# First attention of a two-stage kernel: transposed scores and narrower tiles

## The chip, the cores and the metric

The kernel runs on one core of a Trainium2 chip. The metric is the device time of one execution in microseconds; the time before is the median of two runs. The span of a profile is shorter than the time by what lies around it.

## The reference

For 8 batches and 8 heads, with 576 tokens and 64 columns a head, 32 packed queries p attend over the tokens, and the tokens' queries q attend over the 32 results. The output of all heads, x (576 x 512 a batch), goes through a token mixer:

```python
def sm_attn(qq, kk, vv):
    s = scale * np.matmul(qq, kk.transpose(0, 1, 3, 2))
    a = softmax(s)
    return np.matmul(a, vv)
p_packed = sm_attn(p, k, v)
x = sm_attn(q, p_packed, p_packed)      # heads side by side, [8, 576, 512]
wq, wk = x @ w_q, x @ w_k               # 512 -> 64
W_tok = scale * wq @ wk.T
out = np.maximum(W_tok @ x, 0.0) @ w_out
```

Inputs and output are fp32; the kernel works in bf16 with fp32 sums.

## The kernel before, in words

There is no loop over tiles: the string ORDER lists every step as NAME.batch.part@engine=banks, and the program issues them in just that order. Each engine runs its own steps strictly in the order of the list, so a step that waits holds up all later steps of its engine. A is ScalarE (ACT), V VectorE (DVE), P GpSimd (POOL); steps without an engine are TensorE's, with their PSUM banks after the equals sign. Batches run interleaved, in the order 0, 1, 2, 4, 3, 5, 6, 7. All loads of k, q, v (LD.k3 and so on) and of w_out (LD.O) are issued from POOL's queue, stores (ST, STF) from SP's, and their places stand in the same list. WARM steps are matmuls on zeros that keep the TensorE busy early on.

Four heads lie on the 128 partitions of a k or q tile, each head with 32 groups of 18 tokens. One batch goes through these steps:

- KT: a transpose in blocks of 32x32 on DVE turns k to kT (columns of k on partitions). QV does the same for q, in three parts (two of 512 columns, one of 128).
- S1 (line 261): scores of the packed queries, 32 matmuls in 32x32 tiles, p as weights and 288 tokens moving. The 32 packed queries come out on partitions. X1.b.0 and X1.b.1: exponential on ACT, 576 columns each.
- TE.b.0 and TE.b.1 (step TE, by the helper blocks in line 223): DVE transposes the exponentials, so that tokens are on partitions (tile e).
- PV.b.0 and PV.b.1 (line 282): 36 matmuls in 64x64 tiles, the exponentials of two heads as weights, v with columns of ones beside it moving (192 columns). The ones give the sum for the softmax. In the list, steps of other batches stand between the two parts.
- RC, PP (lines 287, 294): reciprocal of the sum, and the result pp scaled by it and laid out by a mask that puts zeros where another head's block is; PT transposes it to ppT.
- QK (line 306) and QKE: pp times the weights w_q and w_k, 4 matmuls of 192 columns (w_k, w_q, and w_q again), copied to pqk.
- S2, X2, RS, RR, AM (lines 339 to 365): scores of q over the 32 results, exponential, sum, reciprocal and product; AT and AE transpose the product by matmuls with an identity and copy it out.
- WKQ, WE (lines 396, 401): wk for the tokens and wq in the other orientation, from pqk. GM, GE, Y, YE (lines 422, 432): the mixer's small product y. MX and MR (lines 446, 452): the mixed tokens; RL, RLF and RLR apply the relu. RL and RLF write their columns in another order than they read them (function turn).
- OT (line 491): product with w_out, 16 matmuls of 512 columns a batch, and 4 more for the remaining 64 tokens of two batches together; OE and OEF copy it out; ST and STF store it.

k, q and v have four buffers each, e1T, e1, kT and the like two.

Of the kernel before, what the change touches and what calls it, by code (L numbers as in the profile page):

```python
# [7 lines left out]
NL, NB, NO, NE = 4, 3, 10, 2  # L8

ORDER = """  # L10
SET.warm LD.P0 LD.P1 LD.P2 LD.P3 LD.W0 LD.W1 LD.K0 LD.k1 LD.K1 SET.mask@V KC.0@V SET.v0@V LD.v0 PC@V
LD.q0 KT.0.0@V KC.1@A SET.v3@V PX@V KT.0.1@V SET.v1@V WARM.27=0 S1.0=0,1,2,3 SET.idf@V KT.1.2@V
SET.aff@P X1.0.1@A LD.k2 WC.0@P SET.aT0@V TE.0.1@V WARM.4=4 S1.1=4,5,6,7 LD.v1 SET.v2@V X1.1.1@A
X1.0.0@A LD.q1 X1.1.0@A TE.0.0@V LD.v2 SET.aT1@V TE.1.1@V WARM.6=2 PV.0.0=2,3 LD.k4 PV.0.1 QV.0.1@V
WC.1@P QV.0.0@V LD.q2 RC.0.1@V RC.0.0@V PP.0.1@V QV.0.2@V PP.0.0@V PT.0@V LD.k3 KT.2.2@V WARM.9=6
S2.0.2=6,7 S2.0.3=0,1 X2.0.2@A X2.0.3@A SET.idb@V TE.1.0@V RS.0.4@V WARM.5=4 PV.1.0=4,5 LD.O PV.1.1
QK.0=2 RC.1.0@V RC.1.1@V RR.0.4@V S1.2=6,7,0,1 PP.1.0@V AM.0.2@P PP.1.1@V AM.0.3@P PT.1@V WARM.1=3
AT.0.2=3 QV.1.1@V AE.0.2@A QK.1=4 X1.2.0@A SET.aT2@V QV.1.0@V QKE.0@A X1.2.1@A QV.1.2@V WARM.2=5
S2.1.3=6,7 LD.v3 QKE.1@A TE.2.1@V S2.1.2=2,3 AT.0.3=5 X2.1.2@A TE.2.0@V X2.1.3@A AE.0.3@V WARM.1=0
PV.2.0=0,1 RS.1.4@V WKQ.0.0=2,3 WKQ.0.2 WKQ.0.1 PV.2.1 WE.0.2@A RR.1.4@V KT.4.2@V AM.1.2@P WARM.1=4  # L20
GM.0=4 AM.1.3@P GE.0@V RC.2.1@V RC.2.0@V WARM.1=6 Y.0=6 PP.2.1@V S1.4=2,3,4,5 YE.0@V PP.2.0@V
X1.4.1@A MX.0.0=6,7 LD.q3 QV.2.0@V MX.0.1=0,1 RL.0.0@A AT.1.3=4 PT.2@V LD.v4 QV.2.1@V AT.1.2=5
X1.4.0@A AE.1.3@V S2.2.3=6,7 RL.0.1@A LD.q4 QV.2.2@V AE.1.2@V S2.2.2=2,3 KT.3.2@V LD.k5 WKQ.1.0=4,5
X2.2.3@A WKQ.1.1 X2.2.2@A WKQ.1.2 S1.3=0,1,6,7 WE.1.2@A RS.2.4@V QK.2=2 X1.3.1@A GM.1=3 LD.q5
OT.0.2=4,5 X1.3.0@A TE.3.1@V GE.1@A OT.0.0=6,7 RR.2.4@V TE.3.0@V OT.0.3 AM.2.2@V AM.2.3@V OT.0.1
LD.k6 OE.0.1@A TE.4.1@V AT.2.2=3 AT.2.3=0 OE.0.0@A AE.2.2@V Y.1=1 TE.4.0@V PV.3.0=4,5 QKE.2@A YE.1@V
MR.0=6,7 PV.3.1 AE.2.3@V RLR.0@A MR.1=2,3 MX.1.0=6,7 LD.v5 RLR.1@A RC.3.1@V QV.3.1@V WKQ.2.0=0,1
RL.1.0@A MX.1.1=2,3 RC.3.0@V WKQ.2.2 PP.3.1@V WKQ.2.1 PP.3.0@V OT.1.4=6 WE.2.2@A PT.3@V QV.3.2@V
QK.3=7 QV.3.0@V OEF.1.4@A GM.2=4 LD.v6 RL.1.1@V PV.4.0=0,1 ST.1.4 GE.2@A QKE.3@A Y.2=6 PV.4.1 YE.2@V
S2.3.2=4,5 S2.3.3=2,3 RC.4.0@V X2.3.2@A RC.4.1@V PP.4.1@V MX.2.0=6,7 OT.1.2=4,5 PP.4.0@V RL.2.0@A  # L30
QV.4.0@V MX.2.1=0,1 X2.3.3@A QV.4.2@V MR.2=6,7 OT.1.3 PT.4@V QV.4.1@V RLR.2@A RL.2.1@A OT.1.0=2,3
RS.3.4@V OE.1.1@A S2.4.2=6,7 S2.4.3=0,1 OT.1.1 RR.3.4@V X2.4.3@A KT.5.2@V AM.3.3@P OT.2.0=4,5
X2.4.2@A OE.1.0@A RS.4.4@V S1.5=0,1,6,7 OT.2.1 LD.q6 X1.5.0@A AM.3.2@V X1.5.1@A LD.k7 AT.3.3=2
RR.4.4@V QV.5.1@V OE.2.0@A OT.2.2=0,1 AM.4.3@P AE.3.3@V QK.4=3 TE.5.1@V AT.3.2=6 OT.2.3 AE.3.2@A
QKE.4@A KT.6.2@V WKQ.3.0=4,5 AM.4.2@P OE.2.1@A AT.4.3=7 LD.v7 WKQ.3.2 WKQ.3.1 AE.4.3@V AT.4.2=6
S1.6=2,3,0,1 WE.3.2@A AE.4.2@V TE.5.0@V WKQ.4.0=6,7 X1.6.1@A QV.5.0@V GM.3=4 LD.q7 WKQ.4.2 X1.6.0@A
WKQ.4.1 GE.3@V PV.5.0=0,1 TE.6.1@V WE.4.2@A Y.3=5 TE.6.0@V PV.5.1 YE.3@A GM.4=4 RC.5.1@V QV.5.2@V
MX.3.1=2,3 RC.5.0@V GE.4@A MX.3.0=6,7 PP.5.0@V RL.3.1@A PV.6.0=4,5 PP.5.1@V Y.4=0 PT.5@V PV.6.1
RL.3.0@A YE.4@V S2.5.3=2,3 RC.6.1@V RC.6.0@V QK.5=1 PP.6.0@V X2.5.3@A PP.6.1@V OT.3.0=6,7 PT.6@V
QKE.5@A S2.5.2=4,5 QV.6.2@V MX.4.0=2,3 QV.6.1@V MR.3=0,1 X2.5.2@A OT.3.1 RL.4.0@A QV.6.0@V RLR.3@V  # L40
S2.6.2=4,5 RS.5.4@V MX.4.1=2,3 S2.6.3=0,1 X2.6.2@A RL.4.1@A OT.3.4=4 X2.6.3@A RR.5.4@V OT.4.0=2,3
OEF.3.4@V AM.5.3@P OE.3.0@A KT.7.2@V QK.6=5 ST.3.4 ST.1.0 OT.4.1 ST.0.0 ST.1.1 ST.0.1 ST.2.0 ST.3.0
OT.3.2=0,1 RS.6.4@V OE.4.0@A AM.5.2@P AT.5.3=4 QKE.6@A ST.4.0 S1.7=6,7,2,3 ST.2.1 RR.6.4@V AE.5.3@V
AT.5.2=5 AM.6.3@P OT.3.3 X1.7.1@A AE.5.2@A X1.7.0@A WKQ.5.0=2,3 OE.3.1@V OT.4.2=4,5 AM.6.2@P WKQ.5.2
WKQ.5.1 QV.7.2@V ST.3.1 TE.7.0@V AT.6.3=6 WE.5.2@A OT.4.3 AE.6.3@V QV.7.1@V GM.5=7 OE.4.1@A
WKQ.6.0=0,1 GE.5@V AT.6.2=6 TE.7.1@V MR.4=2,3 Y.5=7 WKQ.6.1 AE.6.2@A YE.5@A QV.7.0@V WKQ.6.2 RLR.4@A
PV.7.0=4,5 WE.6.2@A MR.5=6,7 MX.5.0=2,3 PV.7.1 RLR.5@V RL.5.0@A MX.5.1=0,1 GM.6=6 RC.7.1@V RC.7.0@V
PP.7.0@V OT.5.4=7 GE.6@A PP.7.1@V RL.5.1@A PT.7@V Y.6=6 OEF.5.4@V S2.7.0=2,3 YE.6@A S2.7.2=4,5
OT.5.2=0,1 X2.7.2@A ST.5.4 ST.4.1 X2.7.0@A RS.7.2@V S2.7.1=6,7 RS.7.0@V MX.6.1=4,5 MX.6.0=2,3
X2.7.1@A OT.5.3 RR.7.2@V RR.7.0@V RL.6.0@A AM.7.2@P RS.7.1@V OT.5.0=6,7 AM.7.0@V OE.5.1@A RR.7.1@V  # L50
RL.6.1@V QK.7=2 AM.7.1@P AT.7.0=3 ST.5.1 OT.5.1 AE.7.0@A QKE.7@V AT.7.2=0 AT.7.1=1 OE.5.0@A AE.7.2@V
WKQ.7.0=4,5 AE.7.1@V MR.6=2,3 WKQ.7.2 WKQ.7.1 ST.5.0 WE.7.0@V OT.6.0=0,1 WE.7.1@A GM.7=6 OT.6.1
GE.7@A RLR.6@A Y.7=7 OT.6.2=4,5 OE.6.0@V YE.7@A MR.7=2,3 MX.7.1=6,7 ST.6.0 MX.7.0=0,1 RLR.7@V OT.6.3
RLF.7.1.0@A RLF.7.0.1@V RLF.7.1.1@A RLF.7.0.0@V OT.7.4=2 OE.6.1@A OT.7.2=3 OEF.7.4@V ST.6.1 OT.7.3=6
ST.7.4 OEF.7.2@V OT.7.1=7 STF.7.2 OEF.7.3@V OT.7.0=0 STF.7.3 OEF.7.1@V STF.7.1 OEF.7.0@A STF.7.0
# [4 lines left out]
def kernel(  # L60
# [27 lines left out]
    P = 128  # L88
# [65 lines left out]
    wqk = const.tile([P, 2, 2, 3, Dl], bf16)  # L154
    wout = const.tile([P, NJ, D], bf16)
    v_bufs = [const.tile([P, 6, W], bf16, name=f"v_sb{n}") for n in range(NL)]
# [33 lines left out]
    mask = const.tile([P, 4, Dh], bf16)  # L190
    aT_bufs = [const.tile([P, 2, 640], bf16, name=f"aT{n}") for n in range(NB)]

    def setup(n):
        a, z = n.rstrip("0123456789"), n[len(n.rstrip("0123456789")):]
        z = int(z or 0)
        if a == "idf":
            zero(idf)
        elif a == "aff":
            nc.gpsimd.affine_select(out=idf, in_=idf, compare_op=mybir.AluOpType.not_equal,
                                    fill=1.0, base=0, pattern=[[-1, P]], channel_multiplier=1)  # L200
        elif a == "warm":
            zero(warm)
        elif a == "idb":
            nc.vector.tensor_copy(idb, idf)
        elif a == "v":
            nc.vector.memset(v_bufs[z][:, 0:6:5].bitcast(u32), 0x3F803F80)  # L206
        elif a == "mask":
            zero(mask.rearrange("a x d -> a (x d)"))
            for u in range(4):
                nc.vector.memset(mask[quarter(u), u, :], 1.0)  # L210
        elif a == "aT":
            for i in range(2):
                zero(aT_bufs[z][:, i, 512:576])
# [24 lines left out]
    def WC(n, eng, bk):  # L238
# [3 lines left out]
        else:  # L242
            copy(eng, wqk[:, :, :, 1], w32[:, 0])
            copy(eng, wqk[:, :, :, 2], w32[:, 0])

    def KT(b, x, eng, bk):
        kT = new("kT", b, [P, 2, RQ, GQ, 2], pool=epool)
        xs = slice(0, 2) if x == 2 else slice(x, x + 1)
        blocks(kT[:, xs].rearrange("a x r g e -> a (x r g e)").bitcast(u32),
               k_in[b][:, xs].rearrange("a x n -> a (x n)").bitcast(u32))  # L250


    def S1(b, eng, bk):
        T["s1", b] = [ps_all[:, n:n + 2, 0:NT] for n in (bk[0], bk[2])]
        for e in range(2):
            for z in range(4):
                for c in range(4):
                    i, gh = (c + z) // 2 % 2, (c + z) % 2
                    lhsT = pT[quarter(c), 2 * b + i, :, e]
                    rhs = T["kT", b][quarter(c), i, :, gh * 16:(gh + 1) * 16, e]  # L260
                    nc.tensor.matmul(T["s1", b][c // 2][quarter(2 * i + gh), c % 2], lhsT, rhs,  # L261
                                     start=e == 0, stop=e == 1)

    def X1(b, cc, eng, bk):
        e1T = new("e1T", b, [P, C, 2, NT], pool=epool)
        nc.scalar.activation(e1T[:, cc], T["s1", b][cc], EXP, scale=scale)  # L266

    def TE(b, cc, eng, bk):
        e1 = new("e1", b, [P, R, C, 2, L], pool=epool)
        blocks(e1[:, :, cc].rearrange("a r x l -> a x r l"),  # L270
               T["e1T", b][:, cc].rearrange("a x (t r g) -> a x r g t", t=2, r=R))

    def PV(b, c, eng, bk=None):
        if bk:
            T["pv", b] = ps_all[:, bk[0]:bk[1] + 1, 0:4 * Dh]
        vt = v_bufs[b % NL]
        for n in range(5 * c, min(5 * c + 5, R)):
            for cc in range(C):
                for i in range(2):
                    rhs = vt[halves(i), 3 * cc:3 * cc + 3, n * Dh:(n + 1) * Dh]  # L280
# [287 lines left out]
```

## Time and profile before

| | before |
|---|---|
| median of 2 runs | 110.83 us (110.74 to 110.92) |
| span of the profiled execution | 110.1 us |
| TensorE matmuls busy (PE) | 91.8 us, of it 16.0 in WARM |
| VectorE busy (DVE) | 87.7 us |
| ScalarE busy (ACT) | 65.7 us |
| GpSimd busy (POOL) | 39.0 us |
| DMA, mean | 234 GB/s |

A row of the profile gives an engine's busy time, its share of the span and its number of instructions. PE is the matmuls, PEld the weight loads, which overlap them. In the lines of the timeline the columns are start, length of the piece, engine, line, operation, output and input, and how often; a bracket names how long the engine was idle before it and what it waited for. A row of DMA issues gives the size and the time from issue to landing.

### The profile page before, as it was taken

Reading aid. Unit: us, or ns where it says so; the run is one execution under the profiler, and the core shown is the slowest. Engines: PE = TensorE matmul, PEld = TensorE weight load, DVE = VectorE, ACT = ScalarE, POOL = GpSimd, SP = SyncE. Lnnn points to the kernel's source line nnn. Section 1 sums busy time; section 2 is a strip of 40 time slices with the busy share of each in tenths; the row PEclk is TensorE's granted clock in tenths of the full one; section 3 lists DMA queues with packets and bytes.
Section 4 is the critical chain, followed back from the end, with each engine's and each line's share of the span. In section 5 each row is a group of like instructions: output and inputs, shape, how many; then the busy total and the mean of one; then the engine's idle time right before and its main releaser. Section 6 shows DMA issues by size and latency. Waiting matters only on the chain.

```text
span 110.1 us, 3454 instructions
## 1 busy us (share of the span) xinstructions
PE 91.8 (83%) x1465; PEld 50.8 (46%) x1481; DVE 87.7 (80%) x170; ACT 65.7 (60%) x97; POOL 39.0 (35%) x53
## 2 busy tenths in 40 slices
PE   5992079869486778999999999899999999999940
PEld 2340022445264365565635577644567654654410
DVE  3310995999999997999998999998979779839630
ACT  0062025022473599398699979899874998846220
POOL 3070049940843972424006892000853002300000
PEclk9999656999999999999999999999999999999999
DMA  3999999999999999999999999999999998362594
GB/s 105 334 257 230 214 199 143 185 206 203 214 213 207 210 205 215 204 208 217 209 252 210 204 207 215 210 207 210 242 406 406 394 405 338 134 266 92 213 381 174
DMA packets 13167, 25.71 MB, mean 234 GB/s; under 512 B 992, under 2 KB 6112, under 8 KB 13152
## 3 DMA queue, kind: packets, MB, share of 16 engines
q0 software_dynamic: 8960, 14.09, 71.4%
q1 hardware_dynamic: 3456, 10.62, 25.1%
q10 hardware_dynamic: 736, 0.79, 2.5%
q8 instruction: 11, 0.18, 0.6%
q14 instruction: 4, 0.03, 0.1%
HBM read 30.15 MB, written 9.44 MB: 360 GB/s over the span
## 4 chain that ended last, share of the span: by engine, by line
PE 42%; DVE 26%; ACT 13%; DMA 7%; issue 5%; ACTq 2%; POOL 1%; DVEq 0%; POOLq 0%
PE ps L491 21%; DMA p<-in_p_dram 7%; DVE e L223 6%; ACT relu L457 5%; DVE kT L223 5%; DVE rs L354 4%; ACT e L344 3%; PE ps L339 3%; PE ps L282 3%; PE ps L446 2%; PE ps L374 2%; ACT e1T L266 2%; DVE qT L223 2%; DVE pp L294 2%; DVE aT L135 2%
## 5 line engine op out<-in xcount | busy, mean ns | idle before, releaser
L491 PE MATMUL ps<-wout,relu 128*128 128x512 bf16 x120 | 30.0, 379 | 0.7 <-issue 0.3
L365 POOL TENSOR_TENSOR a<-e,rr 128x256 bf16<-128x256 f32 (+2 forms) x13 | 16.0, 1244 | 35.1 <-DVE rr L359 14.9
L457 ACT ACTIVATE relu<-ps 128x1024 bf16<-128x1024 f32 (+1 forms) x14 | 17.1, 1242 | 1.8 <-PE ps L446 1.4
L535 PE MATMUL ps<-warm 128*128 128x512 bf16 x52 | 16.0, 449 | 1.6 <-DVE warm L138 1.2
L491 PEld LDWEIGHTS <-relu 128*128 128x128 bf16 x128 | 11.4, 98 | 12.1 <-issue 1.4
L131 ACT ACTIVATE o<-ps 128x1024 f32<-128x1024 f32 (+1 forms) x13 | 12.8, 996 | 6.5 <-PE ps L491 6.5
L266 ACT ACTIVATE e1T<-ps 128x576 bf16<-128x576 f32 x16 | 9.9, 661 | 11.0 <-PE ps L261 8.7
L344 ACT ACTIVATE e<-ps 128x256 f32<-128x256 f32 (+2 forms) x17 | 11.0, 675 | 6.1 <-PE ps L339 5.9
L354 DVE TENSOR_REDUCE rs<-e 128x40 f32<-128x1280 f32 (+2 forms) x10 | 12.1, 1209 | 1.6 <-ACT e L344 1.5
L177 POOL DMA_DIRECT2D v_sb<-in_v_dram x16 | 10.1, 634 | 8.8 <-DVE v_sb L206 4.0
L223 DVE STREAM_TRANSPOSE e<-e1T 128x576 bf16<-128x576 bf16 x16 | 11.9, 756 | 1.3 <-ACT e1T L266 1.2
L223 DVE STREAM_TRANSPOSE qT<-q_sb 128x512 uint32<-128x512 uint32 (+1 forms) x24 | 12.7, 549 | 0.0
L223 DVE STREAM_TRANSPOSE kT<-k_sb 128x1152 uint32<-128x1152 uint32 (+1 forms) x9 | 10.9, 1207 | 0.0
L535 PEld LDWEIGHTS <-warm 128*128 128x128 bf16 x57 | 5.8, 110 | 9.6 <-issue 4.9
L261 PE MATMUL ps<-kT,pT 32*32 32x288 bf16 x256 | 5.0, 328 | 5.2 <-DVE pT L223 4.8
L339 PE MATMUL ps<-ppT,qT 64*128 64x64 bf16 x320 | 7.3, 190 | 2.1 <-DVE ppT L223 1.1
L282 PE MATMUL ps<-v_sb,e 64*64 64x192 bf16 x288 | 8.6, 247 | 0.5 <-DVE e L223 0.4
L131 ACT ACTIVATE wkq<-ps 128x896 bf16<-128x896 f32 (+1 forms) x8 | 7.0, 878 | 3.0 <-PE ps L401 3.0
L339 PEld LDWEIGHTS <-qT 64*128 64x128 bf16 x320 | 6.1, 94 | 5.7 <-issue 2.5
L374 PE MATMUL ps<-idb,a 128*128 128x128 bf16 x80 | 6.8, 220 | 1.0 <-POOL a L365 1.0
L282 PEld LDWEIGHTS <-e 64*64 64x64 bf16 x288 | 6.0, 106 | 2.9 <-DVE e L223 1.8
L294 DVE SCALAR_TENSOR_TENSOR pp<-ps,rec,mask 128x256 bf16<-128x256 f32 x16 | 7.1, 478 | 0.3
(58 smaller groups left out, 126.4 us busy)
## 6 DMA issues: line engine op xcount, KB each, us to landing
out_dram<-o SPq DMA_DIRECT2D x14, 512.0 KB, 4.5
v_sb<-in_v_dram POOLq DMA_DIRECT2D x16, 288.0 KB, 11.7
q_sb<-in_q_dram POOLq DMA_DIRECT2D x8, 576.0 KB, 12.3
k_sb<-in_k_dram POOLq DMA_DIRECT2D x7, 576.0 KB, 13.7
k<-in_k_dram SPq DMA_DIRECT2D x2, 576.0 KB, 5.1
out_dram<-o_rem SPq DMA_DIRECT2D x4, 256.0 KB, 3.6
out_dram<-o SPq DMA_DIRECT2D x4, 256.0 KB, 2.7
p<-in_p_dram ACTq DMA_DIRECT2D x4, 128.0 KB, 7.9
```

Source lines behind the costliest of these rows:

```text
L131: nc.scalar.activation(o, i, COPY)
L177: nc.gpsimd.dma_start(v_bufs[b % NL][halves(i), 1:5], src)
L223: nc.vector.transpose(o, i)
L266: nc.scalar.activation(e1T[:, cc], T["s1", b][cc], EXP, scale=scale)
L282: nc.tensor.matmul(T["pv", b][halves(cc), i, cc * Dh:(cc + 3) * Dh], lhsT, rhs, start=n == 0, stop=n == R - 1, skip_group_check=True)
L339: nc.tensor.matmul(ps[:, y, t - t0, i], lhsT, rhs, start=e == 0, stop=e == 1)
L344: nc.scalar.activation(e2[:, t0:t1].rearrange("a t (i y n) -> a y (t i) n", i=2, y=2), T["s2", b, c].rearrange("a y t i n -> a y (t i) n") ...
L354: nc.vector.tensor_reduce(rs[:, t0 * H:t1 * H], e2v(b, c), axis=AX, op=ADD)
L365: e.tensor_tensor(a2[:, t0:t1].rearrange("a t i (u l) -> a (t i u) l", l=L), e2v(b, c), T["rr", b][:, t0 * H:t1 * H].to_broadcast((P, (t1 ...
L457: nc.scalar.activation(o, i, RELU)
L491: nc.tensor.matmul(ps, lhsT, wout[:, j, :], start=j == 0, stop=j == NJ - 1)
L535: nc.tensor.matmul(ps, warm[:, 0:P], warm, start=True, stop=True)
```

## The change

- S1 swaps its operands: kT is the weight (32 rows by 64 tokens), p moves (32 columns). Tokens come out on partitions, 64 by 64, so TE is gone. It is 144 matmuls a batch in 32x64 tiles. X1 is one instruction of 1152 columns that writes e1 straight away. KT writes its output in another order of columns.
- PV takes 32 packed queries of one head as weights: 72 matmuls a batch in 64x32 tiles, 128 moving columns (ones and the head's v), in one step.
- RC is one instruction. pp holds two blocks for the two heads of a pair instead of four, so PP, PT and the mask are half as wide. QK works on each pair by itself: 8 matmuls in 64x64 tiles of 128 columns; the second copy of w_q is made by a new step QD on POOL from pqk, right behind QKE in the list.
- QV writes the columns of q in the order of the output, and the relu (RL, RLF) keeps the order: turn is gone.
- The list keeps its order otherwise: the merged steps (X1, PV, RC) stand where one of their two parts stood; loads, stores, WARM and banks are as they were. One of the two blocks of ones in v's buffers is gone, so their memsets are half as long.

The core of the diff:

```diff
     def S1(b, eng, bk):
-        for e in range(2):
-            for z in range(4):
-                for c in range(4):
-                    i, gh = (c + z) // 2 % 2, (c + z) % 2
-                    lhsT = pT[quarter(c), 2 * b + i, :, e]
-                    rhs = T["kT", b][quarter(c), i, :, gh * 16:(gh + 1) * 16, e]
-                    nc.tensor.matmul(T["s1", b][c // 2][quarter(2 * i + gh), c % 2], lhsT, rhs,
-                                     start=e == 0, stop=e == 1)
+        for r in range(R):
+            for e in range(2):
+                for i in range(2):
+                    for c in range(4):
+                        nc.tensor.matmul(ps_all[halves(i), banks[c], r * L:(r + 1) * L],
+                                         T["kT", b][quarter(c), i, r, :, e],
+                                         pT[quarter(c), 2 * b + i, :, e],
+                                         start=e == 0, stop=e == 1, skip_group_check=True)
...
-    def X1(b, cc, eng, bk):
-        e1T = new("e1T", b, [P, C, 2, NT], pool=epool)
-        nc.scalar.activation(e1T[:, cc], T["s1", b][cc], EXP, scale=scale)
-
-    def TE(b, cc, eng, bk):
-        e1 = new("e1", b, [P, R, C, 2, L], pool=epool)
-        blocks(e1[:, :, cc].rearrange("a r x l -> a x r l"),
-               T["e1T", b][:, cc].rearrange("a x (t r g) -> a x r g t", t=2, r=R))
+    def X1(b, eng, bk):
+        e1 = new("e1", b, [P, 2, 2, NT], pool=epool)
+        nc.scalar.activation(e1, T["s1", b], EXP, scale=scale)
...
+    def PV(b, eng, bk):
+        T["pv", b] = ps_all[:, bk[0]:bk[1] + 1, 0:2 * Dh]
         vt = v_bufs[b % NL]
+        for n in range(R):
+            for c in range(4):
                 for i in range(2):
+                    nc.tensor.matmul(T["pv", b][quarter(c), i],
+                                     T["e1", b][halves(i), c // 2, c % 2, n * L:(n + 1) * L],
+                                     vt[halves(i), 0:c + 2:c + 1, n * Dh:(n + 1) * Dh],
+                                     start=n == 0, stop=n == R - 1, skip_group_check=True)
...
     def QK(b, eng, bk):
         for i in range(2):
             for e in range(2):
-                nc.tensor.matmul(ps[:, i], T["ppT", b][:, i, :, :, e].rearrange("a c l -> a (c l)"),
-                                 wqk[:, i, e].rearrange("a x m -> a (x m)"), start=e == 0, stop=e == 1)
+                for y in range(2):
+                    nc.tensor.matmul(ps[halves(y), i],
+                                     T["ppT", b][halves(y), i, :, :, e].rearrange("a x l -> a (x l)"),
+                                     wqk[halves(y), i, e].rearrange("a x m -> a (x m)"),
+                                     start=e == 0, stop=e == 1, skip_group_check=True)
...
+    def QD(b, eng, bk):
+        w = T["pqk", b]
+        copy(eng, w[:, :, 2 * Dl:], w[:, :, Dl:2 * Dl])
...
     def RL(b, i, eng, bk):
-        o = new("relu", b, [P, 2, C, 512], pool=epool)[:, i]
-        turn(eng, o.rearrange("a c n -> a (c n)"), T["mx", b, i].rearrange("a c n -> a (c n)"))
+        relu(eng, new("relu", b, [P, 2, C, 512], pool=epool)[:, i], T["mx", b, i])
```

## The prediction

> **What bounds the kernel now.** I read the page first, then the chain, then the loads and their landings, then the timeline of PE stage by stage.
>
> ```profile
> span 110.1 us, 3454 instructions
> PE 91.8 (83%) x1465; PEld 50.8 (46%) x1481; DVE 87.7 (80%) x170; ACT 65.7 (60%) x97; POOL 39.0 (35%) x53
> ...
> PE   5992079869486778999999999899999999999940
> ...
> DVE  3310995999999997999998999998979779839630
> ...
> DMA  3999999999999999999999999999999998362594
> ```
>
> One slice is 2.75 us, counted from 0. DVE is full from slice 7, PE from about slice 15 (41 us) to slice 37, and the DMA engines from slice 1 to slice 32. So three things look full at once, and what the change relieves (DVE) need not be the one that sets the end.
>
> ```profile
> PE 42%; DVE 26%; ACT 13%; DMA 7%; issue 5%; ACTq 2%; POOL 1%; DVEq 0%; POOLq 0%
> ...
> L223 DVE STREAM_TRANSPOSE e<-e1T 128x576 bf16<-128x576 bf16 x16 | 11.9, 756 | 1.3 <-ACT e1T L266 1.2
> ```
>
> By the chain DVE holds 26% of the path; in order of time its DVE part lies before 71 us, and from 71.15 to 105.84 us the chain is PE almost alone. The second line is the step that the change removes (TE).
>
> ```profile
> 23.70 0.77 POOL L172 DMA_DIRECT2D wout<-in_moe_w_out_dram  x1 [1.11 <-DMA v_sb<-in_v_dram]
> ...
> wout<-in_moe_w_out_dram POOLq DMA_DIRECT2D x1, 512.0 KB, 19.2
> ...
> 43.01 3.62 PE L491 MATMUL ps<-wout,relu 128*128 128x512 bf16 x15
> 43.14 0.70 POOL L185 DMA_DIRECT2D q_sb<-in_q_dram  x1 [2.59 <-DMA wout<-in_moe_w_out_dram]
> ...
> 66.14 0.72 POOL L185 DMA_DIRECT2D q_sb<-in_q_dram  x1
> ...
> q_sb<-in_q_dram POOLq DMA_DIRECT2D x1, 576.0 KB, 13.4
> ```
>
> wout lands at 23.70 + 19.2 = 42.9 us and the first OT runs at 43.0: until there the loads set the pace, whatever DVE does. The last q lands at 66.14 + 13.4 = 79.5. Between them issue plus landing time gives the same small slack: k of batch 6 lands at 63.0 and KT.6 runs at 63.99; v of batch 6 at 68.5 and PV.6 runs at 69.80. From 43 us on PE shows only about 2 us of gaps that no missing matmul record explains (the largest: 0.33 ahead of an MX at 75.06, 0.31 ahead of an MR at 55.67 and of S2 at 71.15). So after 43 us the time is PE's own work, and the loads stop it from being moved much forward.
>
> **What PE work costs.** These stages give the prices:
>
> ```profile
> 80.31 0.19 PEld L261 LDWEIGHTS <-pT 32*32 32x32 bf16 x32
> 80.31 0.49 PE L261 MATMUL ps<-kT,pT 32*32 32x288 bf16 x32
> 80.73 0.29 PE L374 MATMUL ps<-idb,a 128*128 128x128 bf16 x2
> ...
> 23.69 0.78 PE L339 MATMUL ps<-ppT,qT 64*128 64x64 bf16 x40 [0.89 <-DVE ppT L223]
> ...
> 86.46 0.61 PE L282 MATMUL ps<-v_sb,e 64*64 64x192 bf16 x20
> 87.00 0.23 PE L452 MATMUL ps<-wkq,y 64*128 64x64 bf16 x4
> ...
> 73.57 1.04 PE L491 MATMUL ps<-wout,relu 128*128 128x512 bf16 x4
> ```
>
> Line 491: (1.04 - 0.38 for the last one's duration) / 3 = 0.22 us for 512 columns, 0.43 ns a column. S1 (line 261): 32 pairs of load and matmul, from its first to the next stage's first 0.42 us; its loads start (0.19 - 0.09) / 31 = 3.3 ns apart. S2 (line 339): (0.78 - 0.19) / 39 = 15.1 ns a pair on two tiles side by side, so 30 ns a round of each tile: 27.5 for its 64 columns and 2.5 more. PV (line 282): five rounds of four tiles in 0.54 us; 5 x 82 ns (192 columns) and 0.03 for the first weights leave 0.10 for the change of tile form.
>
> **The change, part by part.**
>
> TE goes: 16 x 0.756 = 12.1 us of DVE. RC: 8 fewer of 0.166, 1.3. q's transposes of 128 and 512 take 0.288 and 0.680, 1.02 ns a column; PP and PT each halve 256 columns, 0.13 x 24 = 3.1 together. The four memsets of v halve their 0.538: 1.1. DVE falls from 87.7 to about 70. KT now writes with a stride: bounds 0 (its 1.16 ns an element) and 1.6 us in all (q's 1.33), hidden under what DVE loses.
>
> ACT: X1 as one instruction of 1152 columns; o's 512 and 1024 take 0.598 and 1.029, so 1152 takes 1.14 instead of 2 x 0.661: 1.4 us in all. The relu in plain order is priced by o (1.029) against 1.326: 0.3 x 12. With QKE, ACT loses about 5.5 us. All this is off the path after 43 us, except through the 2 us of gaps on PE.
>
> S1: 144 pairs instead of 32. Eight tiles of 32x64, 18 rounds each. A round is bounded by its weights: 64 columns at 0.43 ns, by S2's surcharge 30 ns. 18 x 30 = 0.54, 0.03 for the first weights, 0.10 to leave: 0.67 instead of 0.42, +0.25. No row shows a run of more than 32 pairs at such a pace, so it has two bounds: 3.3 ns a pair (the S1 of before) gives 0.61, +0.19; 15.1 (S2's, the longest run of pairs) gives 2.17 + 0.13 = 2.30, +1.88. I take 0.67: with eight tiles side by side it is nearest to the old S1 row, whose sixteen tiles took pairs at 3.3.
>
> PV: 72 matmuls of 128 columns on eight tiles: 9 rounds x 57.5 ns + 0.12 = 0.64 instead of 9 x 82 + 0.13 = 0.87, -0.23. PV.3 and PV.7 were cut in two by MR and MX of another tile form (0.54 + 0.46 = 1.00 for PV.7), now in one piece: -0.36.
>
> QK: 8 matmuls of 128 columns on two tiles: 4 x 57.5 + 0.03, and 0.10 for each of two changes of form, 0.46 instead of 4 x 0.083 = 0.33: +0.13.
>
> QD is new on POOL: a copy of 128 x 128 by line 133 (0.42 for 256): about 0.25, bounds 0.1 and 0.42. WKQ waits for it, and so does all behind WKQ on PE. POOL's next AM or load waits behind it; the loads have some 10 us of issued transfers ahead of them (wout's 19.2, v's 11.7), so a delay of 0.3 starves none. QD.4 stands between two AMs: QKE.4 ends at 64.35, AM.4.3 too, so AM.4.2 ends at 65.2 instead of 64.9, still before its AT at 65.59. QD.7 is the one with little cover: WKQ.7 ran at 95.48, right behind QKE.7 (94.82 + 0.54). RL.6.1 ahead of QKE.7 and QKE.7 itself get 0.35 shorter, which pays for it: 0, bounds -0.1 and +0.5.
>
> Before 43 us: the shorter memsets and one wqk copy less let the second k load (15.50, behind idf) and the v load behind it start some 0.5 us earlier, in slices where the DMA moved only 143 GB/s. S1's extra five times 0.25 there lies under the wait for wout. Gain 0.3, bounds 0 and 0.8.
>
> The sum after 43 us: S1 three times (batches 5, 6, 7) +0.75; PV five times, 3 x 0.23 + 2 x 0.36 = -1.4; QK five times +0.65; the gaps -1.0 (bounds 0 and -2.1: the ones ended by DVE and ACT shrink, the others stay). That is -1.0, with -0.3 from before 43 us -1.3. The profiled execution has a span of 110.1 and the median of the runs is 110.83, so 0.7 lies around the span: 110.8 - 1.3 = 109.5.
>
> **The rivals.**
>
> *PE's instructions don't come fast enough.* Place: S1, from its 33rd pair on.
>
> ```profile
> q8 instruction: 11, 0.18, 0.6%
> ```
>
> That is 11 packets of 16 KB for about 2960 PE instructions, one for some 268; 0.6% of 16 x 110.1 us is 0.96 us each, 3.6 ns an instruction or 7.2 a pair. The changed kernel has 2 x 1216 more. Paced so, S1 takes 1.17, three times +0.75: 109.5 + 1.5 = 111.0. At S2's 15.1 it is +1.88 three times, and PV 72 x 15.1 = 1.09 + 0.12 is 1.21 (+0.34 three times, +0.21 twice): 5.6 + 1.4 + 0.65 - 1.3 = +6.4, 117.2. It decides from S1 = 1.10, 6.7 ns a pair, on (slower than before), and from 11.9 ns by over 2%. For it: nothing shows more than 64 instructions in a burst. Against: S2 at 15.1 is explained by its columns. The Trainium skill, TensorE: Matmul & The Clock Gate, "Wait — 56ns, not 53.3ns?", says that matmuls start no closer than about 25 ns however few columns they have; by that S1 would take 144 x 25 ns = 3.6 us, an estimate. S2's 15.1 ns shows that this does not hold across tiles. The Trainium skill, Runtime: NRT & Kernel Launch, "Instruction fetch mechanics", has blocks of 256 instructions fetched while the one before runs; the 16 KB packets agree, and an S1 of 288 instructions is longer than a block.
>
> *DVE did set the pace.* Then its share of the chain comes back: TE 5.7% of 110.1 = 6.3, half of pp's 2%, 1.1: 103.4, or up to 108 if the loads hold part of it. For it: DVE at 9 in every slice to 71 us. Against: the landings above, and PE full after 43.
>
> **How the numbers follow.** Forecast 109.5, chance 0.55, its own range 108.3 to 110.9 (gaps, first part, QD). Instructions too slow, 110.9 to 117.2: 0.31. DVE, 103.4 to 108.3: 0.14. The range of 8 in 10 is 107.6 to 114.5: it leaves out most of the DVE case and the slow end of the first rival. A measurement tells about 2% (108.6, 113.0) from no change. Faster by over 2%: 0.13 of the DVE case and 0.06 of the forecast's own, 0.19. Slower by over 2%: pairs slower than 11.9 ns, or S1s stalled by a late block, 0.23. Within: 0.58.
>
> **What would show it.** Right: DVE near 70 us and ACT near 60 busy, OT's first run still at 42.4 to 43 us, S1 stages of 0.6 to 0.75 us, PV of 0.64, PE full to the end. Wrong: pairs of S1 that slow down after the 32nd, or PE idle in "issue" within S1; an OT that starts well before 42 us; a WKQ that waits for POOL.

## The result, and the profile after

The changed kernel takes 143.29 us (median of two runs, 142.94 to 143.64) against 110.83: 1.293 times as long, with a 95% interval of 1.285 to 1.302. The profiled execution has a span of 141.6 us and its own time is 143.64.

These are the lines of its page that answer to those shown of the kernel before. A slice is now 3.54 us. PEclk is the clock granted to the TensorE, in tenths of full speed; the instruction queue q8 moves PE's instructions in packets of 16 KB.

```profile
span 141.6 us, 5860 instructions
PE 106.5 (75%) x2678; PEld 62.8 (44%) x2697; DVE 76.7 (54%) x146; ACT 62.2 (44%) x89; POOL 41.0 (29%) x60
...
PE   6953673992468659369899778676999888999970
...
DVE  2229340729006869500789785503699547684760
...
PEclk9997558689555995955999999977999999999999
DMA  4999999999929089999299259695006999345375
...
PE 64%; issue 14%; DVE 7%; ACT 5%; DMA 5%; ACTq 1%; DVEq 0%
...
q8 instruction: 21, 0.34, 0.9%
```

DVE and ACT did shrink, by 11.0 and 3.5 us, and now have holes everywhere. PE got longer and has holes too. "issue", the time in which an engine waits for nothing that the profile shows, rose from 5% to 14% of the path, and the instruction packets of q8 from 11 to 21. The DMA row, full to slice 32 before, has empty slices in the middle, and the row of the granted clock has stretches of half speed (mean 0.867). Before, its mean was 0.969:

```profile
PEclk9999656999999999999999999999999999999999
```

The added 31.5 us of span can be laid out on PE alone. Its busy time grew by 14.7 (S1 from 5.0 to 11.9; OT from 33.8 to 36.1, WARM from 16.0 to 18.1 and most others by some per cent at the lower clock; PV fell from 8.6 to 7.6). Its gaps, span less busy time, grew from 18.3 to 35.1, so by 16.8: those ahead of S1 and inside it from 5.2 to 13.7, of PV from 0.5 to 4.1, of AT from 1.0 to 3.7.

Inside the stages the gaps look like this. First the waits of PE that end in "issue" (us in total, times, longest), S1 being line 257, PV line 272, AT line 371 and OT line 485.

```profile
PE ps L257 <- issue: 10.0, 4, 4.2
PE ps L272 <- issue: 4.1, 3, 2.4
PE ps L485 <- issue: 1.7, 6, 0.9
PE ps L371 <- issue: 1.7, 3, 0.7
PE ps L529 <- issue: 0.7, 3, 0.3
```

In the kernel before, the same list has these two.

```profile
PE ps L535 <- issue: 0.3, 1, 0.3
PE ps L491 <- issue: 0.3, 2, 0.2
```

So these waits grew by 17.6 us, from 0.6 to 18.2, where all of PE's gaps together grew by 16.8. Next, PE's timeline around PV.0, S1.2, S1.6 and S1.7.

```profile
22.01 0.51 PE L272 MATMUL ps<-v_sb,e 64*32 64x128 bf16 x26
24.88 0.58 PE L272 MATMUL ps<-v_sb,e 64*32 64x128 bf16 x46 [2.36 <-issue]
...
32.06 0.78 PE L257 MATMUL ps<-pT,kT 32*64 32x32 bf16 x76
37.00 0.77 PE L257 MATMUL ps<-pT,kT 32*64 32x32 bf16 x68 [4.16 <-issue]
...
89.64 1.27 PE L257 MATMUL ps<-pT,kT 32*64 32x32 bf16 x134
92.95 0.23 PE L257 MATMUL ps<-pT,kT 32*64 32x32 bf16 x10 [2.05 <-issue]
...
109.23 1.35 PE L257 MATMUL ps<-pT,kT 32*64 32x32 bf16 x144
110.51 0.28 PE L371 MATMUL ps<-idb,a 128*128 128x128 bf16 x2
```

Two things are to be seen. One stage is cut in two by a wait of 1.4 to 4.2 us, at a different matmul each time (after 26, 76 and 134 here), so no operand of the stage explains it. This happens six times, in four S1s and two PVs. If one counts weight loads and matmuls through the whole stream of PE, the pieces resume at numbers 449, 705, 1217, 2241, 3777 and 4033: each is 193 more than a multiple of 256. Waits of 0.6 to 0.9 us in AT and OT end at such numbers too (1985, 3009, 4801). The second thing: an S1 without a cut, the last one, takes 110.51 - 109.23 = 1.28 us for 144 pairs, not 0.67. The trace has its first 32 weight loads within 0.11 us, and after a pause of 0.1 us the pairs follow at 16 in every 133 ns, 8.3 ns a pair. The part of S1.2 that starts at 37.00 ends up at the same 8.3, although the granted clock was 0.50 there and 1.00 in S1.7.

The knock-on shows in POOL's waits and in the loads.

```profile
POOL pqk L127 <- ACT pqk L125: 36.1, 5, 15.6
```

```profile
90.28 0.72 POOL L179 DMA_DIRECT2D q_sb<-in_q_dram  x1
```

POOL stands at QD until PE has done QK and ACT has copied it, and the loads behind QD are issued that much later: the last q load at 90.28 instead of 66.14. The long run of OT that started at 43.01 starts at 62.46, so 19.5 of the 31.5 us are lost by then.

```profile
62.46 4.83 PE L485 MATMUL ps<-wout,relu 128*128 128x512 bf16 x12 [0.22 <-issue]
```

One more group moved, on DVE; first the kernel before, then the changed one:

```profile
L223 DVE STREAM_TRANSPOSE qT<-q_sb 128x512 uint32<-128x512 uint32 x16 | 10.7, 680 | 0.0
```

```profile
L218 DVE STREAM_TRANSPOSE qT<-q_sb 128x512 uint32<-128x512 uint32 x16 | 16.8, 1071 | 2.2 <-DMA q_sb<-in_q_dram 2.2
```

q's transposes of 512 columns take 1.07 us instead of 0.68. They read the same data in the same order; only the order of writing changed, from steps of 8 bytes to steps of 16.

### The profile page after: what moved, and what is told of

It reads as the page before. It is cut to its first block, busy times and chain, and to the rows that moved or that the text cites. A ratio compares the mean times of both kernels' runs of the same rounds, so it can differ in the third digit from the quotient of the medians.

```text
span 141.6 us, 5860 instructions
## 1 busy us (share of the span) xinstructions
PE 106.5 (75%) x2678; PEld 62.8 (44%) x2697; DVE 76.7 (54%) x146; ACT 62.2 (44%) x89; POOL 41.0 (29%) x60
## 4 chain that ended last, share of the span: by engine, by line
PE 64%; issue 14%; DVE 7%; ACT 5%; DMA 5%; ACTq 1%; DVEq 0%
PE ps L485 21%; PE ps L257 8%; PE ps L529 7%; PE ps L272 5%; DMA p<-in_p_dram 5%; PE ps L371 4%; ACT e L264 4%; PE ps L336 4%; PE ps L398 3%; PE ps L444 3%; PE ps L393 3%; PE ps L419 2%; DVE qT L218 2%; PE ps L297 2%; PE ps L429 1%
## 5 line engine op out<-in xcount | busy, mean ns | idle before, releaser
L257 PE MATMUL ps<-pT,kT 32*64 32x32 bf16 x1152 | 11.9, 203 | 13.7 <-issue 10.0
L529 PE MATMUL ps<-warm 128*128 128x512 bf16 x50 | 18.1, 512 | 3.2 <-ACT e L264 1.3
L218 DVE STREAM_TRANSPOSE qT<-q_sb 128x512 uint32<-128x512 uint32 (+1 forms) x24 | 18.6, 809 | 2.2 <-DMA q_sb<-in_q_dram 2.2
L264 ACT ACTIVATE e<-ps 128x1152 bf16<-128x1152 f32 x8 | 9.1, 1131 | 22.8 <-PE ps L257 15.8
L129 DVE COPY aT<-ps 128x1024 bf16<-128x1024 bf16 (+2 forms) x12 | 5.9, 504 | 23.8 <-PE ps L371 14.5
L485 PEld LDWEIGHTS <-relu 128*128 128x128 bf16 x128 | 11.9, 102 | 14.9 <-issue 5.4
L257 PEld LDWEIGHTS <-kT 32*64 32x64 bf16 x1152 | 10.7, 113 | 16.3 <-issue 12.8
L455 ACT ACTIVATE relu<-ps 128x1024 bf16<-128x1024 f32 (+1 forms) x14 | 13.1, 962 | 2.1 <-PE ps L444 2.1
L127 POOL COPY pqk<-pqk 128x128 bf16<-128x128 bf16 x8 | 2.3, 294 | 37.3 <-ACT pqk L125 36.1
L272 PE MATMUL ps<-v_sb,e 64*32 64x128 bf16 x576 | 7.6, 245 | 4.1 <-issue 4.1
L272 PEld LDWEIGHTS <-e 64*32 64x32 bf16 x576 | 6.0, 99 | 7.2 <-issue 7.0
L398 PE MATMUL ps<-aT,pqk 128*128 128x256 bf16 (+1 forms) x48 | 8.6, 275 | 0.0
```

Of the source, the lines that this page charges most:

```text
L218: nc.vector.transpose(o, i)
L257: nc.tensor.matmul(ps_all[halves(i), banks[c], r * L:(r + 1) * L], T["kT", b][quarter(c), i, r, :, e], pT[quarter(c), 2 * b + i, :, e], st ...
L264: nc.scalar.activation(e1, T["s1", b], EXP, scale=scale)
L272: nc.tensor.matmul(T["pv", b][quarter(c), i], T["e1", b][halves(i), c // 2, c % 2, n * L:(n + 1) * L], vt[halves(i), 0:c + 2:c + 1, n * Dh ...
L398: nc.tensor.matmul(o, pqk[:, i, Dl:], aT[:, i, c0:c1], start=i == 0, stop=i == 1)
L455: nc.scalar.activation(o, i, RELU)
```

## The experiments

The theory after the result: PE's instructions come in blocks of 256, and a block is asked for only when the one before it is entered. Where a block runs off in less time than it takes to get the next one, PE waits in "issue". The packets of q8 fit this: the changed kernel has 21 of them and 21 such boundaries, the kernel before 11 and 11. The rivals: the small tiles are slow in the array; QD holds up POOL and with it the loads; q's slower transposes bind. The expectations of e1_cut6, e2_oldS1, e3_QDact and e1_cut2 for this theory each end 0.3 to 2.3 us below the time measured: it had the cause but put the loss a little too low.

**Many matmuls with the old S1** (e1_cut6). In the kernel before, S1's matmuls are cut in six along the tokens; everything else stays.

```diff
-        for e in range(2):
+        for h, e in [(h, e) for h in range(6) for e in range(2)]:
...
-                    rhs = T["kT", b][quarter(c), i, :, gh * 16:(gh + 1) * 16, e]
+                    rhs = T["kT", b][quarter(c), i, h * 3:(h + 1) * 3, gh * 16:(gh + 1) * 16, e]
+                    o = T["s1", b][c // 2][quarter(2 * i + gh), c % 2, h * 48:(h + 1) * 48]
```

> The kernel before, with each matmul of S1 cut in six along the tokens (48 columns instead of 288): 192 pairs a batch instead of 32, 5522 weight loads and matmuls in all, where before has 2962 and the changed kernel 5394. Nothing else differs: TE, QD, PV, loads are those of before. Theory (PE's instructions are fetched in blocks of 256, and a block takes some 5 us from the entry into the one ahead of it): 22 blocks, so 130 to 150 us, with PE idle in 'issue' within S1 for 1 to 4 us several times, 21 or 22 packets of 16 KB in the instruction queue. Rival 1 (QD in POOL's queue holds back the loads and starves everything): there is no QD here, so 110 to 112. Rival 2 (small matmuls of 32x64 tiles are slow in the array): 192 pairs at the 3.3 ns of before are 0.63 us, +0.3 us a batch, 111 to 114.

Measured: 152.32 us (152.21 to 152.44), 1.369 of the kernel before (1.363 to 1.375). PE's timeline around S1.3, and the instruction queue:

```profile
60.14 1.15 PE L262 MATMUL ps<-kT,pT 32*32 32x48 bf16 x116
65.85 0.81 PE L262 MATMUL ps<-kT,pT 32*32 32x48 bf16 x76 [4.56 <-issue]
```

```profile
q8 instruction: 21, 0.34, 0.9%
```

The stage is cut as in the changed kernel, PE resumes at such numbers again (193 more than a multiple of 256), and the time is worse than the changed kernel's. PE waits 24.8 us in "issue", and S1 is busy for 15.4 us instead of 5.0. Here there is no 32x64 tile, no QD and no new order of q. The number of PE's instructions (5522 instead of 2962) is enough to cause such a loss.

**The changed kernel with the old S1** (e2_oldS1): KT, S1, X1 and TE of before, all else changed; 3602 PE instructions instead of 5394.

```diff
-                        nc.tensor.matmul(ps_all[halves(i), banks[c], r * L:(r + 1) * L],
-                                         T["kT", b][quarter(c), i, r, :, e],
-                                         pT[quarter(c), 2 * b + i, :, e],
...
+                    rhs = T["kT", b][quarter(c), i, :, gh * 16:(gh + 1) * 16, e]
+                    nc.tensor.matmul(T["s1", b][c // 2][quarter(2 * i + gh), c % 2], lhsT, rhs,
...
+    def TE(b, cc, eng, bk):
```

> The changed kernel with KT, S1, X1 and TE of before put back (32 matmuls of 32x32 tiles, transposes on DVE); PV in 64x32 tiles, the narrow pp, QK, QD on POOL, the order of q and the plain relu stay. 3602 loads and matmuls, 14 blocks. Theory (blocks of instructions): most of the 32 us comes back, 110 to 117; what is left is PV's and QK's extra instructions. Rival 1 (QD on POOL): QD is still there, so over 125. Rival 2 (S1's tiles): 108 to 112.

Measured: 117.27 us (116.78 to 118.49), 1.056 of before (1.049 to 1.063). So S1's part is some 26 of the 32 us. The rest still has waits for blocks, now in stages that the change did not touch as well as in PV:

```profile
32.24 0.38 PE L403 MATMUL ps<-aT,pqk 128*128 128x256 bf16 x2
35.26 0.27 PE L398 MATMUL ps<-pqk,aT 128*128 128x64 bf16 x2 [2.64 <-issue]
...
74.06 0.66 PE L277 MATMUL ps<-v_sb,e 64*32 64x128 bf16 x55 [1.72 <-issue]
```

The wait of 2.64 us falls into the middle of WKQ, at instruction 961, again 193 more than a multiple of 256.

**QD off POOL** (e3_QDact): the changed kernel, QD on the engine of QKE.

```diff
-QKE.1@A QD.1@P
+QKE.1@A QD.1@A
```

> The changed kernel with QD right behind QKE on the engine of QKE (ACT, in batch 7 DVE) instead of POOL, so that no load waits behind it. Theory (blocks): the loads no longer starve, but the blocks still set the pace: 21 blocks at 4.5 to 5.3 us from some 13.6 us on, 120 to 140. Rival 1 (QD holds the loads): 109 to 114.

Measured: 141.36 us (140.43 to 142.29), 1.271 of before (1.259 to 1.282). So POOL's stand at QD is worth about 2 us. POOL now waits at AM instead, and the last q load is only 4.9 us earlier than the 90.28 of the changed kernel:

```profile
POOL a L362 <- DVE rr L356: 70.2, 7, 19.1
```

```profile
85.41 0.72 POOL L179 DMA_DIRECT2D q_sb<-in_q_dram  x1
```

The late loads are for the most part a consequence of a late PE, not the cause.

**The order of q alone** (e4_order): the kernel before, with q in the order of the output and the relu in plain order.

```diff
-            blocks(qT[:, i, 0:512].rearrange("a (t y g h) -> a h y t g", t=4, y=2, g=GQ),
+            blocks(qT[:, i, 0:512].rearrange("a (t g h y) -> a h y t g", t=4, g=GQ, h=2),
...
-        turn(eng, o.rearrange("a c n -> a (c n)"), T["mx", b, i].rearrange("a c n -> a (c n)"))
+        relu(eng, new("relu", b, [P, 2, C, 512], pool=epool)[:, i], T["mx", b, i])
```

> The kernel before with one part of the change alone: q's columns in output order, relu in plain order. The page of the changed kernel shows q's transposes of 512 columns at 1.07 us instead of 0.68 (16 of them, +6.2 us of DVE), and the relu at 1.02 instead of 1.33 (12 on ACT, -3.6 us). If DVE's time before 43 us and between batches lies under the loads, -0.5 to +1 us: 110.3 to 111.8. If DVE is on the path, +3 to +6: 114 to 117.

Measured: 116.07 us (114.72 to 117.09), 1.046 of before (1.040 to 1.052). DVE's costliest group, and the first OT on PE:

```profile
L223 DVE STREAM_TRANSPOSE qT<-q_sb 128x512 uint32<-128x512 uint32 x16 | 16.9, 1075 | 0.0
```

```profile
44.32 3.62 PE L490 MATMUL ps<-wout,relu 128*128 128x512 bf16 x16
```

DVE does 16 x 0.39 = 6.2 us more, S2's weight loads wait for qT 5.5 us in all instead of 2.2, and OT begins 1.3 us later. Taken alone this part costs 5 us, on a DVE that is full. What the plain relu saves (1.024 us instead of 1.326, 12 times on ACT) is in this time too; no run has it without the order of q.

**Old S1 and old order** (e5_oldS1_oldorder): e2_oldS1 with the old order of q and the old relu, the diff of e4_order backwards.

```diff
-            blocks(qT[:, i, 0:512].rearrange("a (t g h y) -> a h y t g", t=4, g=GQ, h=2),
+            blocks(qT[:, i, 0:512].rearrange("a (t y g h) -> a h y t g", t=4, y=2, g=GQ),
```

> The changed kernel with S1, X1, TE and KT of before and with the order of q and the turning relu of before; PV in 64x32 tiles, the narrow pp, QK and QD stay: 3602 loads and matmuls. If what was left of e2_oldS1's 117.3 over before is the order of q (e4_order: +4.9), 111 to 113. If PV's 144 instructions still run a block dry (e2_oldS1 shows waits of 2.6, 1.7 and 1.0 us near the block ends 960, 2496, 2752), 113 to 116. If the freed DVE counts for something, under 110.

Measured: 117.06 to 119.44 us in four executions, 1.056 of before (1.045 to 1.067), the same as e2_oldS1. A miss: it lies above all three times expected. With TE back and the old order, what is left of the change is PV in 576 matmuls instead of 288 and in one step, the narrow pp with QK and QD, RC in one instruction, and the shorter memsets; it costs 6 us. And q's slower writes, 5 us by themselves, add nothing here, which fits a PE that waits for blocks meanwhile.

**QD off POOL and old order** (e7_QDact_oldorder): e3_QDact with the old order and relu.

```diff
-QKE.1@A QD.1@P
+QKE.1@A QD.1@A
...
-        relu(eng, new("relu", b, [P, 2, C, 512], pool=epool)[:, i], T["mx", b, i])
+        turn(eng, o.rearrange("a c n -> a (c n)"), T["mx", b, i].rearrange("a c n -> a (c n)"))
```

> The changed kernel with QD on QKE's engine and with the order of q and the relu of before: of the change remain S1 without TE, PV, the narrow pp. Theory (PE's blocks of 256 instructions): DVE and POOL are not what binds, so only 0 to 5 us come back from 141.4: 136 to 141. Rival (the two side costs add up to most of it): under 125.

Measured: 144.65 us (144.23 to 145.08), 1.299 of before (1.286 to 1.312). A miss: 6.2 us less of DVE work and a time 3 us longer than e3_QDact's. That the order does not bind in the changed kernel fits; why it came out slower is open.

**Twice the matmuls of S1** (e1_cut2): as e1_cut6, cut in two; 3474 PE instructions.

```diff
+        for h, e in [(h, e) for h in range(2) for e in range(2)]:
...
+                    rhs = T["kT", b][quarter(c), i, h * 9:(h + 1) * 9, gh * 16:(gh + 1) * 16, e]
```

> The kernel before with each matmul of S1 cut in two (64 pairs a batch, 3474 loads and matmuls): the small dose beside e1_cut6. Theory (blocks): 128 instructions at the measured 4.2 ns are 0.53 us, but 256 of a block still take over 5 us with the rest, but for one or two blocks: 111 to 114. A theory in which each S1 instruction costs the same would give (152.3 - 111.2) x 512 / 2560 = +8.2: 119.4.

Measured: 114.36 us (114.35 to 114.36), 1.027 of before (1.017 to 1.036), so a loss of some 2 to 4%. 512 more instructions cost 3 us and 2560 more cost 41: not a price per instruction, or the first would be 8. It has two waits of over 1 us, one in S1 and one in PV:

```profile
28.96 0.26 PE L262 MATMUL ps<-kT,pT 32*32 32x144 bf16 x8 [2.01 <-issue]
```

```profile
73.04 0.44 PE L282 MATMUL ps<-v_sb,e 64*64 64x192 bf16 x11 [1.10 <-issue]
```

Where a block runs off fast enough there is a wait, and elsewhere little or none.

**Blocks with nothing else** (e10_tail): the kernel before, and behind its last OT 640 matmuls of 8 columns on zeros, that is 1280 instructions, with the loads long done.

```diff
+            elif f[0] == "TINY":
+                for n in range(int(f[1])):
+                    c, d = n % 4, n // 4 % 4
+                    nc.tensor.matmul(ps_all[quarter(d), int(bk.split(",")[c]), 0:8], warm[quarter(c), 0:32],
+                                     warm[quarter(c), 0:8], start=True, stop=True, skip_group_check=True)
```

> The disputed cost by itself: the kernel before, and behind its last OT 640 more tiny matmuls (32x32 tiles, 8 columns of zeros, one weight load each, 1280 instructions, five blocks of 256), which write to PSUM and are read by nobody. They run while only the last stores are under way. If dispatch at the 4.2 ns an instruction of S1's long runs is all that counts, 640 x 8.3 ns = 5.3 us behind the end of PE's work (105.8), about 111 us of span: 111 to 113. Theory (a block is asked for when the one ahead of it is entered, and takes some 5 us or more): runs of 256 instructions with gaps of 2 to 5 us between them, four or five times: 118 to 135.

Measured: 123.55 us (123.03 to 124.06), 1.110 of before (1.096 to 1.124). PE's timeline at the end:

```profile
105.74 1.57 PE L535 MATMUL ps<-warm 32*32 32x8 bf16 x149
109.30 1.16 PE L535 MATMUL ps<-warm 32*32 32x8 bf16 x128 [1.99 <-issue]
112.76 1.18 PE L535 MATMUL ps<-warm 32*32 32x8 bf16 x128 [2.29 <-issue]
116.48 1.18 PE L535 MATMUL ps<-warm 32*32 32x8 bf16 x128 [2.55 <-issue]
120.21 1.00 PE L535 MATMUL ps<-warm 32*32 32x8 bf16 x107 [2.55 <-issue]
```

The runs have exactly 128 pairs, 256 instructions, and start 3.46, 3.72 and 3.73 us apart, though PE needs only 1.2 us for each. These matmuls depend on nothing that still moves. The period of a block is the time to get one. The trace shows what it is made of: each packet starts 1.0 to 1.1 us after PE has passed a boundary, never ahead of it, takes 0.9 to 1.2 us, and PE goes on 1.4 to 1.5 us after its end. The DMA engines were 2 to 3% busy meanwhile. The block entered at 105.81 took 3.5 us as well, with stores keeping them 82% busy.

**The boundaries moved** (e11_shift): e5_oldS1_oldorder with 64 of these small matmuls (128 instructions) ahead of the first S1, where PE waits anyway. **The same on the narrow pp** (e12_ppshift): e9_pp, below, with the same 64.

```diff
-WARM.27=0 S1.0=0,1,2,3
+WARM.27=0 TINY.64=4,5,6,7 S1.0=0,1,2,3
```

> e5_oldS1_oldorder with 64 tiny matmuls (128 instructions, about 0.5 us) in the idle time of PE before the first S1: all later instructions move by half a block, nothing else changes. Theory (blocks): PE's waits near instruction 704 (1.5 us) and 960 (3.2), 2496 (0.9) and 2752 (1.2) of e5_oldS1_oldorder, in S1, WKQ, PV and S2, leave those steps, and new ones stand at 192 + 256k of the new count; the time changes with where they fall, 112 to 119. Rival (those steps wait for data, banks or POOL): the waits stay at the same steps, the time within 0.5 us of 117 to 118.

> e9_pp (111.1, as before) with the same 64 tiny matmuls. It has 3026 instructions, about as many as before, so its blocks last 5 to 10 us each and hardly wait: 110.3 to 112.3 if the place of the blocks matters little there; 108.5 to 110 if e9_pp loses time at a block now and the shift frees it.

Measured: e11_shift 121.26 us (120.81 to 121.86), 1.091 of before (1.080 to 1.102); e12_ppshift 111.44 us, 1.002 of before (0.998 to 1.007). PE's timeline of e11_shift, at WKQ and at an OT:

```profile
33.13 0.22 PE L398 MATMUL ps<-pqk,aT 128*128 128x64 bf16 x2
...
56.95 1.12 PE L494 MATMUL ps<-wout,relu 128*128 128x512 bf16 x3 [3.32 <-issue]
```

WKQ, where e2_oldS1 lost 2.64 us and e5_oldS1_oldorder 3.16 at the same instruction, runs on without a wait, and a wait of 3.32 us appears between MX and OT, where none was, at instruction 1985: 193 more than a multiple of 256. The waits sit on the count, not on the stage. The place of the count decides 4 us here (1.091 against 1.056), more than I expected, and nothing in e12_ppshift, where the blocks are long enough anyway.

**The narrow pp alone** (e9_pp): the kernel before with pp, PP, PT, QK and QD as changed.

```diff
-        pp = new("pp", b, [P, 2, 2, 2 * Dh])
+        pp = new("pp", b, [P, 2, 2, Dh])
...
-        copy(eng, new("pqk", b, [P, 2, 3 * Dl]), T["qk", b])
+        copy(eng, new("pqk", b, [P, 2, 3 * Dl])[:, :, 0:2 * Dl], T["qk", b])
+    def QD(b, eng, bk):
```

> The kernel before with the narrow pp alone: PP, PT and the mask half as wide, QK as 8 matmuls in 64x64 tiles, QD on POOL; S1, TE, PV, RC, the order of q as before. PE: five QKs after 43 us at +0.13, +0.65; DVE -3.3 us. If PE alone counts, 111.3 to 112; if DVE is on the path (as the order of q suggests), 108 to 110; if QD in POOL's queue holds the loads, 112 to 115.

Measured: 111.12 us (110.75 to 112.49), 1.000 of before (0.997 to 1.004).

```profile
PE 91.2 (83%) x1496; PEld 50.1 (46%) x1513; DVE 84.8 (78%) x170; ACT 64.9 (59%) x97; POOL 41.0 (37%) x60
```

DVE falls by 2.9 us to 84.8 and nothing is won. Together with e5_oldS1_oldorder this leaves the new PV, by exclusion, for those 6 us; it was not run by itself.

## Why the prediction was wrong, point by point

- **The supply of PE's instructions, the step that failed.** The first rival named the right place and had the right sign in the profile (11 packets in q8), and "What would show it" named its mark, PE idle in "issue" within S1. But the step priced a packet by its transfer, 0.96 us, 7.2 ns a pair, and took S2's 15.1 ns a pair as the upper bound. Both are prices per instruction. What counts is the time from entering one block to having the next: 3.5 to 3.7 us in e10_tail, and in the changed kernel, where PE waited, 4.8 to 6.5 us with loads or stores running and 3.3 to 3.6 with next to none. In the kernel before, the packets of three blocks start 2.9 to 3.3 us after PE entered the block ahead (26.35 to 29.24, 33.21 to 36.30, 40.32 to 43.62), and the transfer comes only then; over all eleven it is 0.7 to 3.7. Its own blocks last 4.7 us (64.81 to 69.47, the shortest) to 9.8, so that passes almost unseen. An S1 of 288 instructions in 1.28 us is more than one block: six times a boundary inside S1 or PV found the next block not there yet. By the per-instruction measure alone, 8.3 ns a pair against the 6.7 from which the rival was to decide, the loss would have stayed small: 109.5 + 3 x 0.61 = 111.3 us, an estimate. The rule cited from the Trainium skill (Runtime: NRT & Kernel Launch, "Instruction fetch mechanics") has its 256 borne out to the instruction; its word that a crossing is "mostly hidden" holds for the kernel before and not for this one.
- **The part ahead of the first OT.** The prediction let S1's extra time there lie under the wait for wout and took a gain of 0.3 us. The changed kernel's wout lands at about 40.3 us (issued at 22.62, 17.7 to landing), yet the long run of OT starts only at 62.46, 19.5 us later than before. So it is not the wait for wout that sets the pace there. PE's waits at block boundaries come to 11.1 us up to then, and five S1s, each 0.86 us longer than before, add about 4.3, an estimate.
- **The rival's upper end.** It gave 117.2, and the range 114.5, because a stall by a late block stood in the chances only as a word, without a price. Priced by the 3 us that the trace of before has between a boundary and its packet, with the transfer behind it, it would have been some 4 us a block, an estimate that still leaves out the 1.3 to 1.5 us from the packet's end to PE's next instruction.
- **S1's term, mis-sized as well.** 0.67 us was added up from the columns, and chosen because it lay nearest to the old S1, whose 32 pairs went at 3.3 ns. Past the 32nd pair the pace is 8.3 ns a pair in S1, and the same in e10_tail with 8 columns, where columns can't explain it. The stage takes 1.28 us where nothing waits: +0.86 instead of +0.25. PV's 72 pairs take 0.73 (68.44 to 69.17) instead of the 0.64 of the sum.
- **q's order, left out of the sum.** The prediction gave KT's new stride bounds and gave QV's none. KT's group keeps its duration (1.345 us for 1152 columns, before 1.337, steps of 8 bytes); q's goes from 0.68 to 1.07 us at steps of 16 bytes. By itself this is 5 us (e4_order); where PE waits for blocks, taking it out gave nothing back (e5_oldS1_oldorder, e7_QDact_oldorder). The Trainium skill, Advanced Engine Details and Errata, "SBUF Cachelines", has lines of 16 bytes of which two hits are needed for full speed; steps of 8 give two, steps of 16 give one, and the two durations agree.
- **QD at nothing.** Right as far as it goes: e3_QDact is 2 us below the changed kernel, where the prediction allowed 0.5. The 36 us that POOL waits at it are for the most part PE's lateness handed on.
- **DVE's relief worth little.** This held for what was tried alone (e9_pp, 2.9 us for nothing). TE's 12.1 us were not taken out by themselves. The other direction is not free: 6.2 us more cost 5 (e4_order).
- **The durations of the other engines.** These were near: X1 1.131 us (1.14 predicted), relu 1.023 (1.03), QD 0.294 (0.25), PP and PT together 3.4 us less (3.1), ACT 62.2 in all (60). DVE has 76.7 instead of 70, and most of the difference is q's 6.2.
- **Not told apart.** The waits in "issue" are shown to come from the blocks: of their 18.2 us, 16.0 end at a boundary and lie in the nine waits named above. S1's own pace makes another 6.9 us. The rest, 7.8 us of PE time, lies in stages that the change hardly touched and that took longer while the granted clock was lower. Why the clock fell, and what the late loads cost by themselves, no run here shows.

## What to carry to other kernels

Count the instructions of PE, weight loads included, and look how long the shortest 256 in a row take: in this case a block below some 5 us began to cost, and one of 1 to 2 us cost 2 to 5.5 us of waiting. Trading a transpose on another engine for more than four times as many small matmuls is a trade against that supply, which no busy time shows beforehand; packets in the instruction queue and their distance from the boundaries do. When a layout changes, price the strides of every write, also of those where only an order of columns moved.

## What the runs showed of the hardware

- A block of 256 PE instructions (one 16 KB packet) takes 3.46 to 3.73 us from one to the next with the DMA engines 2 to 3% busy (e10_tail), of which the packet's transfer is 0.9 to 1.2. Where PE waited in the changed kernel, it took 4.8 to 6.5 us with loads or stores running. What makes a packet start later among other transfers, no run separates: with stores alone one block took 5.2 us (entered at 109.58 in the changed kernel) and another 3.5 (at 105.81 in e10_tail). Only one packet seems to be on its way at a time: in e10_tail each starts only after PE has entered the block that the one before it brought.
- In a dense stage the first 32 pairs of load and matmul go in 0.11 to 0.15 us (S1.7, and S1.2 from 37.00 on), the rest at 8.3 ns a pair, whatever the columns (8 in e10_tail, 32 in S1) and at a granted clock of 0.50 as at 1.00.
- DVE transposes of 32-bit data in 32x32 blocks, 512 columns: 0.68 us when written in steps of 8 bytes, 1.07 in steps of 16.
